# Conformer block on one core: GpSimd instead of VectorE computes the statistics of 15 LayerNorms

## The chip, the core and the metric

The kernel runs on one core of a Trainium2 chip. A core has TensorE (PE, matrix products into PSUM), VectorE (DVE), ScalarE (ACT), GpSimd (POOL) and SyncE (SP, which here only issues DMAs). The engines run side by side, each in the order of its own instruction list, and wait for each other on semaphores. The metric is the device time of one execution in microseconds; a change is told faster or slower here from 0.2% on.

## The reference

Input and output are 2 sequences of 4000 tokens with 144 channels, bf16. All weights are bf16; `_layernorm` takes mean and variance over the 144 channels and has no gain or bias.

```python
h = _layernorm(x);  x = x + 0.5 * (_silu(h @ w_ff1a) @ w_ff1b)      # 144 -> 576 -> 144
h = _layernorm(x);  q, k, v = split(h @ w_qkv)                     # 4 heads of 36
x = x + softmax(q k^T * 36**-0.5) v  @ w_o
h = _layernorm(x);  a, b = split(h @ w_pw1);  h = a * sigmoid(b)
x = x + _silu(depthwise_conv5(h)) @ w_pw2
h = _layernorm(x);  x = x + 0.5 * (_silu(h @ w_ff2a) @ w_ff2b)
return _layernorm(x)
```

So there are five LayerNorms for each token, and the attention over 4000 keys is most of the work.

## The kernel before

The 8000 tokens are 16 chunks of 500; a chunk is four blocks of 125 tokens, with tokens on the partitions. The running sum x stays in SBUF as `X`, bf16, [125 partitions, 64 blocks, 144].

**Attention.** For each chunk of queries the kernel walks over 63 tiles of 64 keys. PE makes the scores into two PSUM banks (`PS<-QT,KT`), then either ACT takes the exponential of both banks in one instruction (`ACT ... PT<-PS`), or DVE does it in five: two conversions from PSUM (`PT<-PS`, 128x500) and three steps within SBUF called y, m and w (`PT<-PT`: an and/or, a product of two tensors, an and/or). Then PE adds `PT` times the values to a sum in PSUM (`PS<-PT,VA`). 215 tiles are done by DVE, the others by ACT.

**Everything else** (feed-forward, projections, convolution, norms) is woven between these tiles. A norm is the function `ln(c, bs)`. For a whole chunk in the middle of the run it does the following: DVE issues two `bn_stats`, each over two blocks (125x288 bf16), which write count, mean and sum of squared deviations of each row into `ST`; GpSimd computes variance plus epsilon (`RS`), raises it to the power -0.5 (`NHALF`), negates the mean, and scales the four blocks of `X` into `XN` (125x144 each). After that SP issues a DMA transpose into `XTB`, from which PE multiplies, or, for the last norm of a chunk, the store to DRAM. `bn_stats` reads each pair of blocks interleaved, so that its two groups of three values are those of the two blocks.

**What sets the order.** The functions are coroutines that a planner runs with its own costs to make a first list of operations. Then `settle()` rewrites it by tables in the file: `UNITS` has one letter for each movable piece of work (`R.unit`), which says on which engine it runs (p for GpSimd, d for DVE, a for ACT), and `ORDER` gives for each engine the place of every step. `Rec.choose` applies the letters, `Rec.arrange` the order, `Rec.finish` finds the semaphore waits that are needed. The planner's costs so have no say in the final order. Instructions of one engine that depend on one another also wait on a semaphore. Since all are issued by one helper, every row of the profile carries the same line, L589.

Buffers that matter: `ST` and `RS` have five slots, as `XN`; `TH` holds the tanh tiles, six slots, of which two belong to `ff_wide` (two feed-forward tiles at once; the program as built has no such tile); `DWR` is a small buffer for the raw depthwise weights, used once near the start of the middle part (`setup_dw`).

Of the kernel before, what the change touches and what calls it, by code (L numbers as in the profile page):

```python
# [6 lines left out]
ALU = mybir.AluOpType  # L7
# [161 lines left out]
        '+8#v#y#z+9#{+5+:+;#|+<+=#}$!+>+?+@$#+A+B+C+D$&$$$%+E+F+G$(+H+J+I$)$*+K+O+L+P+M+N+Q$++T+R+U$,+S+V+Z+Y'
        '+W+X+[$-+]+^+_+`$.+a$/+e+b+d$0$3+f+c$4$1$2+g+j+i+k+h+l$6+m$7+n+o$5+p+s+q+t$8+u+x+v+r,!$9+w+}+y,,,#,&'  # L170
        ',-,$,%$:,.,($;,/,0+z,)$<+{+|$>$=,*,1$?,+,2,7,6,3,8,4,5$@$A,9,;,<,:,=,@,>,A$C,B,?,E,C,F,D,G,J$D$E,K$F'
        ',H,L,I$G,M,O,N,P$H,T$I,U,V$J,W$K,X,Q$L,R$M$N,S$O,Y$B,Z$P,[,_,],^$Q$R,`,a,d$S,e,b$T,c,f$U$V,i,g,j$W,k'
        ',n$X,h,l,o$Y,p,m,q$Z$[,s$],t,r,u,x$^,v,y$_,w,z,}$`,{-!$a-#-&$b-$-(,|-)-%-*-,$c---+-.$d-/-1-0$e-2-3$g'
        '-4$j$f-5$h-6$i-7-8-;$k-9-<$l-:-@-=$m$n-A->-B-E$o-?$p-C-F-D$q-G-J-H-K$r-O-I-L-P-M-Q$s-N-R-T$t-U-S-V-Y'
        '-W-X-Z$u-[-_-]-`-^$v-d-a-l-b-c-e$w-i-j-f-k-g-m-h$y-r-n-s-o-t-p-q$z${-u-v-w$|%)-x$}$x-y%!-z%,-{%#-|-}'
        '.!%$%%.%.&.(%&.).#.$%+%*.*%(.+%-%..,%/.-.0%0...1./%2%3%4%5.5.6.2.7.8.3.9.4.:%6.;%1.?.<%7.=.@%8.>.D.A'
        '%9.E.F%:.G.B.C%=%;%<.J.I.N%>.K.H.O%?%@.L.M%B.P%A.Q%C.T.S.R%D%F%E.U.X.V.Y.W.Z%G.[%H%I._.c.]%K.d.^%J.`'
        '.h.a%L.e%M.i.f.m%N.g%O.n.b.j.r.k.o.s.p%P.l%Q.w.q%R.x.}.y.|.z.t/%.u%S/&.{/+/!.v/,/#/(/$/)%T/0/5/*/-/.'
        '%U/1/6///2/7/3%V/4%W%X/8%Y/9%[%Z/?/:/@/;/<%^/A%`/B%_/=%a/>%b/C/D%c%]%e%d/E%f/F/I/G/J%g/H/O/N/K%h/S/L'
        '/P/Q/T%i/M/U/X/R/Y%j/V%k/W/Z/^/[%l/]%m/_/`/c/a/b%n/d/h/i/m/n/j/o/p/k/e%p/f%o/q/s/r/l/t/u/g/v%q%r/w/x'  # L180
        '0$0#%s0%/y/|%t/}0!0*0&/z%u0+/{0(0)0/%w040,%v050-%x060.00070801%y020:%z03%{090>0;%|0<0?0=0@%}0A0C0D0B'
        '&!0E&#0H0F&$0G&%0I0J&&0K0R0L0S&(0W0M0N0T0O0U0V0P&+&)&*0X0^0]0Q0_0Y0`0a&,0b0c0Z0d0[0e&-0g0f0h0m0l0q0i'
        '0r0n0j0o&.0v&/&00p0w0k0{0|0s0t0u&1&21$0}1!1#1%0x&30y&41&0z1(1/1)1+1*1,&61015111-1.&712&813&5141:1619'
        '171;181<1=&91?1>1C1D1@1E1A1B1I1H1F1G&;1J&:1K&<&>&=&?1R&@1L1M1N1O1S1P1T&A1Q1U1V1W1X&B1Y1]1^1Z1b1_1[1`'
        '1c&C1d1g1e1h1a1i1l1j1m&D1n1f1o&E1t1p&F1q1k1r1s&G&H&J&I&K1z1{1|&L&M1}1u1v2#2!1w2$1x1y2)&N&O2*2+2,2%2-'
# [8 lines left out]
        '5:(l5>55(k5A5?5F5@5B5E(p5G(o5C5P5D(q(i5H(m5O(n(t5U(r5Q5I(s(u5T5R5V5S5W5`5X5K5J5_5L5a5M5b(v(w5N5c5Y5Z'
        '5[5]5^(j(x)#(y(z)%({(})&(|)!)*))).)$)D)<)F)()=)>)+),)-)/)E)B)L)1)M)0);)?)I)@)2)N)C)4)5)3)G)7):)6)J)8'
        ')P)O)K)A)9)Q)H)U)V)R)S)T)Y)X)W)])Z)^)_)`)b)a)c)[)e)d)f)g)l)i)j)k)h)m'
# [124 lines left out]
class Rec:  # L321
# [441 lines left out]
def bass_standalone__conformer_family_zipformer__speech_kernel(  # L763
# [28 lines left out]
    def sb(name, shape, dt=BF16):  # L792
        return nc.alloc_sbuf_tensor(name, [128] + list(shape), dt)

    NXN, NXT, NTH, NHT, NSW = 5, 5, 6, 3, 3
# [27 lines left out]
        "FFW": (  # L823
# [4 lines left out]
        ),  # L828
# [140 lines left out]
    RS = sb("RS", [NXN, 3, NB], F32)  # L969
    NHALF = sb("NHALF", [NB], F32)  # L970
# [35 lines left out]
    DWR = sb("DWR", [D + 64])  # L1006
# [135 lines left out]
    def now(k):  # L1142
# [7 lines left out]
        Slots(R, range(n)) for n in (NXN, NXT, NTH - 2, NHT, NSW, NAN, NPT))  # L1150
    thw = Slots(R, [NTH - 2])
# [87 lines left out]
    def ln(c, bs, e=False, store=False):  # L1239
# [9 lines left out]
        calm = small(c)  # L1249
        if n == NB and not calm and not store and ("XN", u) not in clear:  # L1250
# [164 lines left out]
    def ff_wide(s, h, m, WA, nm):  # L1415
        bks, t = yield need("pe", (wide, thw), dur=0.84)
        for j in range(2):
            mm2(WA, s, (m + j) * 128, (m + j) * 128 + 128, bks[j], 128, [(nm, "a", 0)])
        yield need("act")
        rk = [("ps", bks[0]), ("ps", bks[1]), "TAB0"]  # L1420
        ps = PSV[:, bks[0]:bks[0] + 2, 0:CH]
        op("act", "activation", TH[:, t:t + 2, :], ps, ACT.Tanh, bias=0.0, scale=0.5, r=rk, w=[("TH", t)],
           cost=c_act(2 * CH))
        yield need("dve", hold=True)
        op("dve", "scalar_tensor_tensor", out=HT[:, h, m:m + 2, :], in0=TH[:, t:t + 2, :], scalar=1.0, in1=ps,
           op0=ALU.add, op1=ALU.mult, r=[("TH", t)] + rk, w=[("HT", h)], cost=c_dve(2 * CH))
        banks.give(bks[0])
# [1081 lines left out]
```

## Time and profile before

| what | value |
|---|---|
| median of 3 runs | 868.13 us (868.13 to 868.39) |
| profiled execution, time | 868.3 us |
| profiled execution, span from first to last instruction | 866.5 us |
| granted TensorE clock, mean | 0.998 |
| busy: PE, DVE, ACT, POOL | 849.1, 833.6, 835.0, 278.9 us |
| `bn_stats` on DVE | 160 instructions, 65.6 us |
| scaling into `XN` on POOL | 250 instructions, 141.6 us |

The profile's page gives busy times, the chain of work that ended last (followed back from the last instruction, at each step to what released it), and groups of equal instructions with their count, busy time, mean duration, and the engine's idle time just before them. Other views give the same for a window, or the instructions in order of time. An operand is written out<-in with the program's names.

### The profile page before, as it was taken

To read this page: it belongs to the slowest core of one execution; us is meant where nothing else is said; L and a number is where in the kernel's file an instruction comes from. 1 tells how busy PE (TensorE), PEld (TensorE's weight loads), DVE (VectorE), ACT (ScalarE), POOL (GpSimd) and SP (SyncE) were. 2 spreads that over 40 slices of the span, in tenths; PEclk is the share of its full clock that TensorE was granted. 3 is DMA by queue.
4 is the path that set the end of the run, shared out by engine and by line. 5 is a ranking of instruction groups with operands and counts; after the bars stand their busy time and mean duration, and the time that the engine had idled before them with its cause. 6 is when DMAs were issued, how large, how long until landed. Compare 5 with 4: busy or idle time off the path is not lost.

```text
span 866.5 us, 27023 instructions
## 1 busy us (share of the span) xinstructions
PE 849.1 (98%) x11585; PEld 411.2 (47%) x11585; DVE 833.6 (96%) x1819; ACT 835.0 (96%) x1096; POOL 278.9 (32%) x562
## 2 busy tenths in 40 slices
PE   9999999999999999999999999999999999999996
PEld 7644434444344444444444444444444544445485
DVE  7989999999999999999999999999999999999986
ACT  6999999999999999999999999999999999999975
POOL 7661331041334301432230060330550163300854
PEclk9999999999999999999999999999999999999999
DMA  3320211102113110212210020010130021100121
GB/s 103 87 56 14 33 21 38 21 14 45 34 26 51 14 26 2 40 31 45 34 39 2 2 44 3 17 29 14 27 47 6 5 54 37 29 2 14 36 51 51
DMA packets 86554, 26.95 MB, mean 31 GB/s; under 512 B 81607, under 2 KB 86433, under 8 KB 86433
## 3 DMA queue, kind: packets, MB, share of 16 engines
q1 hardware_dynamic: 84884, 24.38, 15.3%
q8 instruction: 91, 1.49, 0.7%
q10 hardware_dynamic: 1548, 0.84, 0.4%
q14 instruction: 31, 0.25, 0.1%
HBM read 3.34 MB, written 2.30 MB: 7 GB/s over the span
## 4 chain that ended last, share of the span: by engine, by line
ACT 40%; PE 40%; DVE 16%; DMA 1%; POOL 1%; issue 1%; DVEq 0%; POOLq 0%; ACTq 0%
PE PS L589 40%; ACT PT L589 37%; DVE PT L589 11%; ACT TH L589 3%; DVE ST L589 1%; DVE QT L589 1%; DVE X L589 1%; POOL XN L589 1%; DVE HT L589 1%; DVE U L589 1%; DMA XTB<-XN 0%; DMA X<-in_x_dram 0%; DMA out_dram<-XN 0%; DVE KT L589 0%; POOL RS L589 0%
## 5 line engine op out<-in xcount | busy, mean ns | idle before, releaser
L589 ACT ACTIVATE PT<-PS 128x1000 bf16<-128x1000 f32 (+1 forms) x793 | 730.2, 1070 | 5.3 <-PE PS L589 4.3
L589 PE MATMUL PS<-QT,KT 64*64 64x500 bf16 x3968 | 460.3, 383 | 4.3 <-ACT PT L589 1.2
L589 PE MATMUL PS<-PT,VA 64*37 64x500 bf16 x4828 | 449.5, 372 | 1.3 <-DVE QT L589 0.6
L589 DVE TENSOR_SCALAR PT<-PS 128x500 int16<-128x500 f32 x425 | 279.7, 678 | 4.4 <-PE PS L589 3.1
L589 PEld LDWEIGHTS PS<-QT,KT 64*64 64x64 bf16 x3968 | 139.7, 104 | 201.6 <-ACT PT L589 98.9
L589 PEld LDWEIGHTS PS<-PT,VA 64*37 64x37 bf16 x4828 | 163.1, 96 | 105.8 <-issue 16.4
L589 POOL TENSOR_SCALAR RS<-ST 125x4 f32<-125x4 f32 (+1 forms) x132 | 31.2, 238 | 482.2 <-DVE ST L589 478.5
L589 DVE TENSOR_SCALAR PT<-PT 128x1000 uint16<-128x1000 uint16 x430 | 172.3, 419 | 1.8 <-DVE PT L589 0.2
L589 DVE TENSOR_TENSOR PT<-PT 128x1000 bf16<-128x1000 bf16 x215 | 144.9, 678 | 0.8
L589 POOL TENSOR_SCALAR XN<-X,RS 125x144 bf16<-125x144 bf16 x250 | 141.6, 578 | 4.3 <-POOL RS L589 0.9
L589 POOL TENSOR_TENSOR RS<-RS,NHALF 125x4 f32<-125x4 f32 (+2 forms) x93 | 91.9, 993 | 53.5 <-DVE RS L589 51.4
L589 ACT ACTIVATE TH<-PS 128x500 bf16<-128x500 f32 (+3 forms) x175 | 92.8, 560 | 3.8 <-PE PS L589 3.4
L589 DVE SCALAR_TENSOR_TENSOR HT<-TH,PS 128x500 bf16<-128x500 bf16 (+1 forms) x120 | 71.7, 617 | 1.4 <-ACT TH L589 1.0
L589 PE MATMUL PS<-XTB,WA 72*128 72x500 bf16 (+2 forms) x280 | 71.1, 359 | 0.8 <-DMA XTB<-XN 0.2
L589 DVE BATCH_NORM_STATS2 ST<-X 125x6 f32<-125x288 bf16 (+1 forms) x160 | 65.6, 449 | 1.8 <-DMA X<-in_x_dram 1.1
L589 DVE SCALAR_TENSOR_TENSOR X<-PS,X 125x288 bf16<-125x288 f32 x114 | 50.9, 452 | 7.0 <-PE PS L589 5.9
L589 PE MATMUL PS<-WB,HT 128*125 128x144 bf16 (+1 forms) x640 | 52.2, 229 | 0.1
L589 PEld LDWEIGHTS PS<-WB,HT 128*125 128x125 bf16 (+1 forms) x640 | 45.0, 136 | 13.4 <-issue 3.9
L589 PEld LDWEIGHTS PS<-XTB,WA 72*128 72x128 bf16 x280 | 21.5, 97 | 29.0 <-issue 8.3
L589 PE MATMUL PS<-U,DG 128*128 128x375 bf16 (+7 forms) x204 | 28.0, 263 | 0.2 <-DVE RD L589 0.2
L589 POOL COPY U<-U 128x2 bf16<-128x2 bf16 (+1 forms) x54 | 10.8, 234 | 42.2 <-DVE U L589 32.1
L589 ACT ACTIVATE HT<-PS 128x500 bf16<-128x500 f32 (+3 forms) x43 | 20.6, 537 | 3.4 <-PE PS L589 2.9
(95 smaller groups left out, 513.9 us busy)
## 6 DMA issues: line engine op xcount, KB each, us to landing
X<-in_x_dram SPq DMA_DIRECT2D x16, 140.6 KB
XTQ<-XTB SPq DMA_DIRECT2D x24, 70.3 KB
out_dram<-XN SPq DMA_DIRECT2D x12, 140.6 KB
XTB<-XN SPq DMA_TRANSPOSE x53, 3.2
out_dram<-XN ACTq DMA_DIRECT2D x2, 140.6 KB
XTB<-AN SPq DMA_TRANSPOSE x15, 3.2
WA<-in_w_ff1a_dram ACTq DMA_DIRECT2D x1, 144.0 KB
WB<-in_w_ff1b_dram ACTq DMA_DIRECT2D x1, 144.0 KB, 2.6
```

What stands on the lines that cost most here:

```text
L589: ins = getattr(eng, o.name)(*o.a, **o.k)
```

## The change

In the LayerNorms of whole chunks in the middle part, a third letter, s, is now possible for the two `bn_stats`. With it DVE issues neither, and GpSimd makes the same two statistics (mean into `ST[..., 1]`, sum of squared deviations into `ST[..., 2]`) itself: it squares both halves of the 144 channels, adds the halves, adds the channels pairwise 72, 36, 18, 9 down to one, and corrects the sum of squares by the square of the sum over 144. Squares and plain sums go side by side as eight columns of 72 in `SQ`, fp32. 15 of the letters are s. The new list stands in GpSimd's order ahead of the `RS` instruction that reads `ST`.

The place for `SQ` and `SS` comes from `TH` (six slots to four; `ff_wide` is removed with its policy) and from `DWR`, which becomes a view of `SQ`; a norm can have the letter s only when `setup_dw` is done with that. The tables of PE, ACT and SP are untouched; those of DVE and POOL have new numbers, because the count of their steps changed, and name the remaining instructions in the order of before.

```diff
@@ Rec.choose
+                if code == "s":
+                    o.deps += [(x, True) for x in more]
                 more.append(o)
@@ buffers
-    NXN, NXT, NTH, NHT, NSW = 5, 5, 6, 3, 3
+    NXN, NXT, NTH, NHT, NSW = 5, 5, 4, 3, 3
+    SQ = sb("SQ", [2 * NB, HD], F32)
+    SS = sb("SS", [3, NB], F32)
-    DWR = sb("DWR", [D + 64])
+    DWR = SQ[:, :, :].rearrange("p i d -> p (i d)").bitcast(BF16)
@@ ln
+        seen = [(d, True) for j in range(n) for d in R.history(("X", c, b0 + j))[0]]
+        raws = []
         for j in range(0, n, 2):
-            op("dve", "bn_stats", ST[0:rows, u, j:j + 2, :].rearrange("p i k -> p (i k)"),
+            o = op("dve", "bn_stats", ST[0:rows, u, j:j + 2, :].rearrange("p i k -> p (i k)"),
...
+            raws.append(o)
         calm = small(c)
+        if n == NB and not calm and not e and R.history("DWR2")[1]:
+            seen += [(d, False) for q in ("DWR", "DWR2") for h in R.history(q) for d in h]
+            lo, hi = (X[0:TB, c * NB:c * NB + NB, q:q + HD] for q in (0, HD))
+            s1, s2, s3 = SS[0:TB, 1, :], SS[0:TB, 0, :], SS[0:TB, 2, :]
...
+            more = [(SQ[0:TB, NB:2 * NB, :], hi, hi, ALU.mult, 0.9), (SQ[0:TB, 0:NB, :], lo, lo, ALU.mult, 0.9),
+                    (SQ[0:TB, 0:NB, :], SQ[0:TB, 0:NB, :], SQ[0:TB, NB:2 * NB, :], ALU.add, 0.9),
+                    (SQ[0:TB, NB:2 * NB, :], lo, hi, ALU.add, 0.9), (z(0, 36), z(0, 36), z(36, 72), ALU.add, 0.9),
+                    (z(0, 18), z(0, 18), z(18, 36), ALU.add, 0.6), (z(0, 9), z(0, 9), z(9, 18), ALU.add, 0.42),
+                    (z(0, 3), z(0, 3), z(3, 6), ALU.add, 0.3), (z(0, 3), z(0, 3), z(6, 9), ALU.add, 0.3),
+                    (SS[0:TB, 0:2, :], col(0), col(1), ALU.add, 0.3),
+                    (SS[0:TB, 0:2, :], SS[0:TB, 0:2, :], col(2), ALU.add, 0.3), (s3, s1, s1, ALU.mult, 0.25)]
+            R.unit(raws, "d", {"s": [
+                ("pool", "tensor_scalar", (ST[0:TB, u, :, 1], s1, 1.0 / D, None), dict(op0=ALU.mult), 0.25, None),
+                ("pool", "tensor_tensor", (ST[0:TB, u, :, 2], s2, s3), dict(op=ALU.add), 0.25, None)]},
+                   {"s": [("pool", "tensor_tensor", (a, b, d), dict(op=f), t, None, None, seen) for a, b, d, f, t in more] + [
+                       ("pool", "tensor_scalar", (s3, s3, -1.0 / D, None), dict(op0=ALU.mult), 0.25, None, None, seen)]})
@@ ff: ff_wide removed
-        nw = 0 if silu or mode["front"] else now("FFW")
-        kids = S.spawn([ff_wide(s, h, 2 * j, WA, nm) for j in range(nw)] + [
-            ff_tile(s, h, m, WA, WE, nm, silu) for m in range(2 * nw, 5)])
+        kids = S.spawn([ff_tile(s, h, m, WA, WE, nm, silu) for m in range(5)])
```

(The last numbers in the rows of `more` are the planner's costs.)

More of the change, by code (lines that the diff above doesn't have):

```diff
@@ L169 @@
[L169 to L173, printed above, removed]
@@ L194 @@
[L194 to L196 removed]
+        '#,#-#.#V)_)`#/)a)b#0#1)d)e#2)f)i)g#4)c#3#5)h)j)k)l#7#6#W)t)n)m)o)s)p#8)q#9)u#:)v)w)r#<)x)y)})z#;#=*!'
+        '){*#)|*(*$#>*&*%#?*)#@***+*,*-*1*.#A*/*0#B*2*3#C#D#F*6#E*4*7*5#G#H*;#I*8*9*<*=*:*>*?#J*A*@*E*F*B#K#L'
@@ new lines @@
+        '#M*C*D#N#Y*J*G#O#P#R*K#Q#S*H#^*L#T#X*I*M#Z*N*P#[#_*O*Q#]*R*S#a*U#`*T#b#c*V*Y*W*Z*X*[#e*_*]#f#g*^*`#h'
+        '*a#i*b*d#j*c*e#d#k*f*j*g*i*h*k#m*l#l*m#n#p*n*o*s#o*p*x#q*q*y*t*}*u*r#r*v#s*z#t+!#u*w+&*{*|+#+$#v#w+('
+        '+)#x#y+*#z+%+++,#{+-+.#|#}+/+0+1$!+2+3+4+5$%$#$$+6+7+8$&+9+;+:$($)+<+@+=+A+>+?+B$*+E+C+F$++D+G+K+J+H'
+        '+I+L$,+M+N+O+P$-+Q$.+U+R+T$/$2+V+S$3$0$1+W+Z+Y+[+X+]$4+^$5+_+`+a+d+b+e$6+f+i+g+c+o$7+h+n+j+x+p+s+y+q'
+        '+r$8+z+t$9+{+|+k+u$:+l+m$<$;+v+}$=+w,!,(,&,#,),$,%$>$?,*,,,-,+,.,1,/,2$@,3,0,6,4,7,5,8,;$A,<$B,9,=,:'
@@ L197 @@
+        '4D4E(G4F(I4G4:4H(J4J4K4L4I(K4O4M4N4P4T4Q(L4R4U4S4V4Y4W(M4_4`4X4a4Z4b4c4[4e(N4]4d4^4f4g(O4j4h4i(Q4k4l'
+        '(P4m(R(S4o4n4p(T4q(U(V4s4t4u4r4v4w(W(X4y4x5(4z4}4{4|5-5&5,5!5)5#5*5.5$5+(]5/5%([525057515356(a58(`54'
+        '5A55(b(Y59(^5@(_(e5F(c5B5:(d(f5E5C5G5D5H5P5I5<5;5O5=5Q5>5R(g(h5?5S5J5K5L5M5N(Z(i(p(j(k(r(l(n(s(m(o(v'
+        '(u(z(q)5)-)7(t).)/(w(x(y({)6)3)=(})>(|),)0):)1)!)?)4)$)%)#)8)()+)&);)))A)@)<)2)*)B)9)F)G)C)D)E)J)I)H'
+        ')M)K)N)O)P)R)Q)S)L)U)T)V)W)])Y)Z)[)X)^'
     ),
@@ L206 @@
+        '#Y#[#a#b#f#c#`#k#d#g#e#m#i#l#n#o#p#r#q#s#x#y#}#z#t#{$+#|$$$&$!#w$)#u$#$%#v$($*$,$-$.$:$4$2$3$/$0$5$8'
+        '$6$7$1$9$;$<$=$A$>$B$C$?$D$E$G$F$@$I$H$J$K$L$Q$S$U$O$T$P$V$W$X$Y$M$_$]$N$Z$[$^$a$e$c$R$b$d$f$`$g$h$j'
+        '$i$n$r$p$q$s$t$u$v$k$x$y$w$l$z${$m$|$o%!%#%$%%%&%(%*%)%+$}%,%-%.%/%1%0%2%3%4%5%6%<%=%>%7%?%8%@%D%E%A'
+        '%:%G%F%9%H%;%B%I%C%K%L%J%O%U%R%V%M%W%X%S%N%P%Q%T%Y%Z%]%^%[%_%`%a%b%c%d%f%e%g'
     ),
@@ L1149, in bass_standalone__conformer_family_zipformer__speech_kernel @@
     xnp, xtp, thp, htp, swp, anp, ptp = (
-        Slots(R, range(n)) for n in (NXN, NXT, NTH - 2, NHT, NSW, NAN, NPT))
-    thw = Slots(R, [NTH - 2])
+        Slots(R, range(n)) for n in (NXN, NXT, NTH, NHT, NSW, NAN, NPT))
     wide = Wide(banks)
@@ L1413, in ff_tile @@
         thp.give(t)
[L1415 to L1427, printed above, removed]
-        banks.give(bks[1])
-        thw.give(t)
     def ff(c, s, WA, WE, WB, nm, silu, then):
         h = yield need("pe", htp)
-        nw = 0 if silu or mode["front"] else now("FFW")
-        kids = S.spawn([ff_wide(s, h, 2 * j, WA, nm) for j in range(nw)] + [
-            ff_tile(s, h, m, WA, WE, nm, silu) for m in range(2 * nw, 5)])
+        kids = S.spawn([ff_tile(s, h, m, WA, WE, nm, silu) for m in range(5)])
         yield need("pe", kids=kids)
```

69 lines of the change are left out of this document (32 added, 37 removed), and 4 rows, old and new, of the table POLICY.

## The prediction

> **What bounds the kernel now.** I read the page first (busy shares, the chain that ended last, the costliest groups), then busy time by stretch, then the chain in the stretches where the change acts, then single tiles and timelines.
>
> ```profile
> span 866.5 us, 27023 instructions
> PE 849.1 (98%) x11585; PEld 411.2 (47%) x11585; DVE 833.6 (96%) x1819; ACT 835.0 (96%) x1096; POOL 278.9 (32%) x562
> ACT 40%; PE 40%; DVE 16%; DMA 1%; POOL 1%; issue 1%; DVEq 0%; POOLq 0%; ACTq 0%
> L589 DVE TENSOR_SCALAR PT<-PT 128x1000 uint16<-128x1000 uint16 x430 | 172.3, 419 | 1.8 <-DVE PT L589 0.2
> L589 DVE TENSOR_TENSOR PT<-PT 128x1000 bf16<-128x1000 bf16 x215 | 144.9, 678 | 0.8
> L589 DVE BATCH_NORM_STATS2 ST<-X 125x6 f32<-125x288 bf16 (+1 forms) x160 | 65.6, 449 | 1.8 <-DMA X<-in_x_dram 1.1
> XTB<-XN SPq DMA_TRANSPOSE x53, 3.2
> ```
>
> Three engines are full at once, and the chain changes between them: 40% of it is ScalarE's (ACT), 40% TensorE's (PE), 16% VectorE's (DVE). GpSimd (POOL) has two thirds of the span free. In the body, by stretch:
>
> ```profile
> 40.00:820.00 780.00, 772.04 (x10720) 351.37 (x10718) 763.73 (x1599) 771.51 (x963) 228.29 (x453) 1.00 0.15 27
> ```
>
> The columns are PE, its weight loads, DVE, ACT, POOL. ACT is idle for 8.5 of 780 us, DVE for 16.3. ACT's share cannot shrink, since the change takes nothing from it; so no relief of DVE can give more than ACT's idle time there.
>
> **What the change removes.** 15 norms lose their two bn_stats on DVE: 30 x 449 ns = 13.5 us of DVE's 833.6. The orders of PE, ACT and SP stay as they are, and so does DVE's but for the missing 30; the wide feed-forward tile that goes is issued nowhere, and the smaller TH and the move of DWR into SQ add no instruction: nothing for them, by that order.
>
> **What it adds.** 15 GpSimd instructions a norm, 225 in all: five of 288 elements, one of 144, one of 72, two of 24, two of 8, four of 4. The trace has no addition of two tensors on GpSimd, so I bound it.
>
> ```profile
> L589 POOL TENSOR_SCALAR XN<-X,RS x250: 452/460/1740, 16.1 to 857.2; 125x144 bf16<-125x144 bf16 x125
> L589 POOL MEMSET XN<- x5: 465/471/472, 17.7 to 71.1; 128x448 bf16 x5
> L589 POOL TENSOR_SCALAR RS<-ST x132: 187/221/699, 5.5 to 855.6; 125x4 f32<-125x4 f32 x113, 125x2 f32<-125x2 f32 x18, 126x2 f32<-126x2 f32 x1
> 145.25 0.20 POOL L589 TENSOR_SCALAR RS<-ST 125x4 f32<-125x4 f32 x1 [22.76 <-DVE ST L589]
> 145.53 1.01 POOL L589 TENSOR_TENSOR RS<-RS,NHALF 125x4 f32<-125x4 f32 x1
> ```
>
> The first three rows give min/median/max in ns. From below, an instruction that only writes: 471/448 = 1.05 ns an element, 0.30 us for 288. From XN, which reads one tensor: (460-187)/140 = 1.95 ns an element over a fixed 187 ns, 0.74 us for 288. From above, that slope twice, for two tensors read in full: 1.29 us. I take 0.80 us, close to XN, the nearest row (same engine, same rows of X, two arithmetic steps), a little over it for the second operand. [...]
>
> At 2.16 ns an element over 187 ns (0.80 us for 288), a norm costs 5 x 0.80 + 0.49 + 0.33 + 2 x 0.23 + 2 x 0.20 + 4 x 0.19 = 6.4 us; each instruction waits for the one before it, and such a wait costs 0.08 us (145.25 + 0.20 to 145.53), 14 times: 7.6 us (about 4.6 to 10.4 between the ends). GpSimd goes from 279 to about 393 us busy, 45%.
>
> **Does anyone wait for the later statistics?** Today GpSimd waits for them:
>
> ```profile
> POOL RS L589 <- DVE ST L589: 478.5, 58, 35.9
> ```
>
> That is 478.5 us in 58 waits, 8.2 us each, and the new work starts in that idle time, as soon as the chunk is written and GpSimd is free. For the 15 places that is at 155.7, 197.2, 222.1, 241.0, 273.4, 298.9, 323.3, 360.0, 401.5, 429.3, 473.8, 530.3, 592.7, 667.0 and 785.3 us. In about half of them the statistics are then ready before bn_stats ended, in the others up to 7 us later. The tightest place is the eighth:
>
> ```profile
> 360.94 0.81 DVE L589 BATCH_NORM_STATS2 ST<-X 125x6 f32<-125x288 bf16 x2
> 363.15 2.54 POOL L589 TENSOR_SCALAR XN<-X,RS 125x144 bf16<-125x144 bf16 x4
> 369.00 1.27 SPq L589 DMA_TRANSPOSE XTB<-XN  x1
> 380.08 0.58 PE L589 MATMUL PS<-XTB,WA 72*128 72x500 bf16 x2
> ```
>
> The block ends at 360.0 + 7.6 = 367.6 instead of 361.75, 5.9 us late. The XN behind it in GpSimd's queue (of another chunk) ends at 371.6, SP's transpose goes out at 371.6 instead of 369.0, lands 3.2 us later (page row above) at 374.8, and PE uses it at 380.08: 5.3 us to spare. SP has nothing else to issue until this has landed. So the added latency is put at nothing; it is hidden by GpSimd's idle time and this slack.
>
> **The cost on VectorE.** GpSimd and VectorE get in each other's way:
>
> ```profile
> 441.45 0.90 POOL L589 TENSOR_SCALAR XN<-X,RS 125x144 bf16<-125x144 bf16 x2
> 442.05 0.83 DVE L589 TENSOR_TENSOR PT<-PT 128x1000 bf16<-128x1000 bf16 x1
> L589 DVE TENSOR_SCALAR PT<-PT x430: 365/414/690, 56.6 to 820.1; 128x1000 uint16<-128x1000 uint16 x144
> L589 DVE TENSOR_TENSOR PT<-PT x215: 627/672/859, 57.2 to 819.4; 128x1000 bf16<-128x1000 bf16 x108
> ```
>
> The product at 442.05 began with 0.30 us of a GpSimd instruction to go (441.45 + 0.90 = 442.35) and took 0.83 us instead of the median 0.672: it lost what was left of that instruction less 0.15 us. What this costs now: mean less median, (419-414) x 430 + (678-672) x 215 = 3.4 us, against 250 x 0.460 = 115 us of undisturbed XN, so 3.0%. An instruction of length T makes a VectorE one that starts at random lose (T-0.15)^2/2T: 0.104 us for XN, 0.264 for 0.80 us, 2.5 times. So 7.6% of 15 x (4.0 + 0.49 + 0.33) = 72 us: **5.5 us of lock losses** on VectorE. (At 0.30 us an instruction: 0.3 us; at 1.29: 16.7.) The short instructions, about 0.2 us, cost next to nothing.
>
> [...]
>
> **What reaches the end.** Two of the 15 pairs lie on the chain, 0.73 us each:
>
> ```profile
> 289.52 1.46 DVE ST L589 x4
> 432.55 0.73 DVE ST L589 x2
> by line: DVE PT L589 74.2%; PE PS L589 17.4%; DVE HT L589 6.5%; DVE X L589 4.1%; issue 0.5%
> by line: ACT PT L589 41.0%; DVE PT L589 25.7%; PE PS L589 21.1%; ACT TH L589 5.3%; DVE AN L589 5.1%; issue 3.4%; DVE RD L589 2.7%
> by line: DVE PT L589 80.4%; PE PS L589 13.2%; DVE U L589 10.0%; issue 1.0%
> by line: DVE PT L589 52.6%; DVE ST L589 16.2%; DVE QT L589 11.2%; DVE VA L589 6.6%; DVE KT L589 6.5%; DVE HT L589 6.5%; DVE X L589 4.3%; issue 1.0%
> 155.70:164.70 9.00, 9.00 (x146) 3.93 (x140) 8.90 (x20) 9.00 (x11) 1.45 (x3) 1.00 0.16 31
> ...
> 785.30:794.30 9.00, 9.00 (x144) 4.89 (x138) 9.00 (x19) 9.00 (x12) 0.20 (x1) 1.00 0.16 32
> sum 135.00, PE 133.54 PEld 58.09 DVE 133.15 ACT 134.97 POOL 18.29; mean PE 8.90 PEld 3.87 DVE 8.88 ACT 9.00 POOL 1.22
> ```
>
> Two of the four instructions at 289.52 are of a norm that moves. The four "by line" rows are the chain in 222.1:231.1, 298.9:307.9, 401.5:410.5 and 429.3:438.3, the only ones of the 15 stretches (9 us each) in which it runs over DVE: 85%, 34%, 90% and all, 28 of 135 us. The last rows are busy times over the 15 stretches (first, last and sum): DVE is idle for 1.85 us of 135, ACT for 0.03.
> - Gain: 2 x 0.73 = -1.46 us. The other 13 pairs are off the chain; taking them out frees DVE, and nobody was waiting there.
> - Loss on the chain: 5.5 x 28/135 = +1.1 us.
> - Loss elsewhere: 4.4 us in stretches where ACT has no idle time. DVE's own idle time there, 1.85 x 107/135 = 1.5 us, takes its part; the rest delays what PE gets from DVE, and ACT through PE, and an engine without idle time does not make that up: +2.9 us.
>
> Sum: +2.5 us on the profiled execution's 868.3 us, which lies 0.2 us over the median of 868.13: **870.6 us**, slower by 0.3%. Between the ends of the lock losses it would be -1.4 us (0.3 us lost, all of it hidden) to +13.8.
>
> **The rivals.** *The relief reaches the end (faster).* DVE is freed of 13.5 - 5.5 = 8.0 us. TensorE waits for it, and ACT for TensorE:
>
> ```profile
> PEld PS L589 <- DVE PT L589: 72.7, 239, 0.6
> ACT PT L589 <- PE PS L589: 4.3, 13, 0.6
> ACT TH L589 <- PE PS L589: 3.4, 10, 1.4
> ```
>
> If a third of the 8.0 us comes out of ACT's 8.5 us of idle time in the body, that is -2.7 us, 865.4. It decides from 1.7 us on (0.2% of 868, about what a measurement can tell from no change). For it: 239 waits of weight loads on DVE's exponentials. Against: near the removed pairs ACT is not idle at all.
> *Hidden (no change).* The losses off the chain fall into DVE's waits: -1.46 + 1.1 = -0.4 us, 867.7. For it: at most 0.4 us per block. Against: DVE's 0.12 us of idle time a stretch.
> *GpSimd comes too late (slower).* It decides when a block takes 7.6 + 5.3 = 12.9 us, beyond the upper end; each us more is then a us of PE's wait at 380. At 15 us: +2 on top, 872.7.
> That the change does nothing is excluded: in the built program bn_stats go from 160 to 130, and GpSimd gains 225 instructions.
>
> **How the numbers follow.** Forecast (losses pass): 0.50, of which 0.06 at small losses stay within 0.2%; relief reaches the end: 0.25; hidden: 0.21; too late: 0.04. So faster 0.25, same 0.27, slower 0.48. The range reaches down past a third of the relief, 865.0, and up to twice the losses (11 us: -1.46 + 2.3 + 7.2 = +8.0), 876.3. The forecast's own range is 868.5 to 876.3.
>
> **What would show it.** DVE busy falls by 8 us (13.5 less 5.5), PT<-PT means rise from 419 and 678 ns to about 426 and 690 (430 x 7 + 215 x 12 = 5.6 us), medians stay; the 288-element rows take 0.80 us; GpSimd's waits for DVE ST shrink; ACT's idle time in the body grows by 2 to 3 us. Wrong: if those means stay, if ACT's idle time falls under 8, or if PE waits for XTB at 380.

## The result, and the profile after

The changed kernel takes 879.33 us (median of 4 runs, 879.28 to 879.52) against 868.26 us for the kernel before in the same session: a ratio of 1.0127 (95% interval 1.0109 to 1.0144), slower by 1.3%. The prediction said slower, but by 0.3%, and 879.3 lies outside its range. The profiled execution's span is 877.5 us, at the same granted clock as before (0.998).

The page of the changed kernel: busy times, the chain that ended last by engine, and the costliest groups that matter here (group rows: out<-in, shapes, count | busy us, mean ns | idle before them).

```profile
span 877.5 us, 27220 instructions
PE 852.3 (97%) x11585; PEld 411.0 (47%) x11585; DVE 840.5 (96%) x1789; ACT 837.8 (95%) x1096; POOL 392.4 (45%) x787
...
PE 42%; ACT 30%; DVE 27%; issue 1%; DMA 0%; POOL 0%; DVEq 0%; ACTq 0%
...
L592 DVE TENSOR_SCALAR PT<-PT 128x1000 uint16<-128x1000 uint16 x430 | 183.3, 444 | 2.1 <-PE PS L592 0.6
L592 DVE TENSOR_TENSOR PT<-PT 128x1000 bf16<-128x1000 bf16 x215 | 150.7, 705 | 0.8
L592 DVE BATCH_NORM_STATS2 ST<-X 125x6 f32<-125x288 bf16 (+1 forms) x130 | 53.5, 448 | 1.6 <-DMA X<-in_x_dram 0.9
```

GpSimd went from 279 to 392 us (forecast: 393). VectorE should have come down by 8 us; it went up by 7, from 833.6 to 840.5, although 30 `bn_stats` are gone. The two `PT<-PT` groups took that back and more: their means rose from 419 to 444 ns and from 678 to 705 ns (forecast: 426 and 690). VectorE's share of the chain went from 16% to 27%.

One tile's rows (min/median/max in ns) show that the instructions as such are what they were; it is the longest that grew, from 690 and 859 ns:

```profile
L592 DVE TENSOR_SCALAR PT<-PT x430: 368/414/1050, 56.5 to 832.0; 128x1000 uint16<-128x1000 uint16 x144
L592 DVE TENSOR_TENSOR PT<-PT x215: 626/672/1549, 57.1 to 831.2; 128x1000 bf16<-128x1000 bf16 x108
```

Mean less median, (444-414) x 430 + (705-672) x 215, is 20.0 us. It was 3.4 us before, so 16.6 us are new. The work that GpSimd gained, shapes kept apart:

```profile
L592 POOL TENSOR_TENSOR SQ<-X 125x288 f32<-125x288 bf16 x45 | 34.5, 767 | 136.7 <-DVE X L592 113.2 <-ACT X L592 21.2
L592 POOL TENSOR_TENSOR SQ<-SQ 125x288 f32<-125x288 f32 x30 | 27.6, 919 | 2.4
L592 POOL TENSOR_TENSOR SQ<-SQ 125x144 f32<-125x144 f32 x15 | 8.2, 546 | 1.2
L592 POOL TENSOR_TENSOR SQ<-SQ 125x72 f32<-125x72 f32 x15 | 5.7, 383 | 1.2
```

The five 288-element instructions take 0.77 and 0.92 us, 0.83 on the mean (the shortest 0.66 and 0.79): the forecast's 0.80 was near. Who waits (waiting engine and tile <- what it waited for: us, times, longest):

```profile
POOL RS L592 <- DVE ST L592: 226.9, 42, 22.8
PEld PS L592 <- DVE PT L592: 86.1, 253, 1.8
ACT PT L592 <- PE PS L592: 12.7, 26, 1.5
```

GpSimd's wait for `bn_stats` halves, from 478.5 us. What grows is what stands behind VectorE: weight loads waiting for its exponentials (72.7 to 86.1 us), and ScalarE's exponentials waiting for TensorE (4.3 to 12.7 us). In the body ScalarE is now idle for 791.0 - 773.5 = 17.5 us, where it was 8.5:

```profile
40.00:831.00 791.00, 774.13 (x10711) 350.31 (x10713) 769.66 (x1568) 773.45 (x961) 340.70 (x676) 1.00 0.14 26
```

(Columns: PE, weight loads, DVE, ACT, POOL.) A single loss looks like this, in order of time:

```profile
227.35 0.85 POOL L592 TENSOR_TENSOR SQ<-SQ 125x288 f32<-125x288 f32 x1
...
227.47 1.27 DVE L592 TENSOR_TENSOR PT<-PT 128x1000 bf16<-128x1000 bf16 x1
```

The GpSimd addition ends at 227.35 + 0.85 = 228.20. VectorE's product, begun at 227.47, takes 1.27 us instead of 0.67: it lost 0.60 of the 0.73 us that were left. The trace has 35 `PT<-PT` instructions that ran beside a wide sum and took over 25 ns more than their median; 34 of them lost what was left of the sum less 0.13 to 0.14 us.

Since ScalarE's order is untouched, the start of its n-th exponential can be set against the same one before, which shows where the time went. The table is worked out from the traces (start after, less start before, us; relief, powers and few are experiments below):

```
start before   changed   relief   powers    few
156.4           -0.2       0.3      0.8     0.0
176.0            0.9       0.3      0.8     0.0
216.4            1.9       0.3      0.8    -0.1
236.2            4.0       0.4      0.8    -0.1
276.7            5.2       0.4      0.8     0.0
336.8            8.0      -0.1      0.0    -0.5
395.0            7.8      -0.1      0.2    -0.5
434.6            9.1       0.5      0.4     0.8
532.6           10.9       0.5      0.4     0.9
608.7           11.5       0.7      0.6     0.9
808.7           11.9       0.5      0.3     1.3
```

The delay climbs where the norms with GpSimd's sums lie (eight of the fifteen between 155 and 361 us), stands still between them, and is never made up.

### The profile page after: what moved, and what is told of

Read it like the earlier page. It is cut to its first block, busy times and chain, and to the rows that moved or that the text cites. A ratio compares the mean times of both kernels' runs of the same rounds, so it can differ in the third digit from the quotient of the medians.

```text
span 877.5 us, 27220 instructions
## 1 busy us (share of the span) xinstructions
PE 852.3 (97%) x11585; PEld 411.0 (47%) x11585; DVE 840.5 (96%) x1789; ACT 837.8 (95%) x1096; POOL 392.4 (45%) x787
## 4 chain that ended last, share of the span: by engine, by line
PE 42%; ACT 30%; DVE 27%; issue 1%; DMA 0%; POOL 0%; DVEq 0%; ACTq 0%
PE PS L592 42%; ACT PT L592 27%; DVE PT L592 20%; ACT TH L592 2%; DVE HT L592 1%; DVE ST L592 1%; DVE QT L592 1%; DVE X L592 1%; DVE U L592 1%; DMA X<-in_x_dram 0%; DVE KT L592 0%; DVE AN L592 0%; DVE XN L592 0%; POOL RS L592 0%; DVE VA L592 0%
## 5 line engine op out<-in xcount | busy, mean ns | idle before, releaser
L592 ACT ACTIVATE PT<-PS 128x1000 bf16<-128x1000 f32 (+1 forms) x793 | 730.4, 1054 | 13.8 <-PE PS L592 12.7
L592 DVE TENSOR_SCALAR PT<-PT 128x1000 uint16<-128x1000 uint16 x430 | 183.3, 444 | 2.1 <-PE PS L592 0.6
L592 DVE TENSOR_TENSOR PT<-PT 128x1000 bf16<-128x1000 bf16 x215 | 150.7, 705 | 0.8
L592 POOL TENSOR_SCALAR RS<-ST 125x4 f32<-125x4 f32 (+1 forms) x132 | 33.1, 253 | 231.7 <-DVE ST L592 226.9
L592 POOL TENSOR_TENSOR SQ<-X 125x288 f32<-125x288 bf16 x45 | 34.5, 767 | 136.7 <-DVE X L592 113.2
L592 ACT ACTIVATE TH<-PS 128x500 bf16<-128x500 f32 (+3 forms) x175 | 90.9, 548 | 4.5 <-PE PS L592 4.1
L592 DVE BATCH_NORM_STATS2 ST<-X 125x6 f32<-125x288 bf16 (+1 forms) x130 | 53.5, 448 | 1.6 <-DMA X<-in_x_dram 0.9
L592 POOL TENSOR_TENSOR SQ<-SQ 125x288 f32<-125x288 f32 (+2 forms) x90 | 50.0, 556 | 7.1
L592 PEld LDWEIGHTS PS<-WB,HT 128*125 128x125 bf16 (+1 forms) x640 | 45.0, 136 | 13.5 <-issue 4.3
```

The source lines that it names most:

```text
L592: ins = getattr(eng, o.name)(*o.a, **o.k)
```

## The experiments

Three theories for the 11 us stood at first. Theory 1: GpSimd's wide instructions hold up VectorE's `PT<-PT` (what the prediction calls lock losses, at three times the forecast 5.5 us; the traces show who is held up and for how long, not by what). Theory 2: GpSimd is late with the norms, and somebody waits. Theory 3: taking `bn_stats` out, or the smaller `TH` and the shared `SQ`, does harm by itself. All runs were timed beside the kernel before on the same chip; ratios are to it.

**Relief alone** (`relief`). `bn_stats` are gone, and GpSimd writes constants instead of the sums. Theories 1 and 2 had 864 to 868 us here, theory 1 with the `PT<-PT` means back at 418 to 421 and 677 to 682 ns.

```diff
-            more = [(SQ[0:TB, NB:2 * NB, :], hi, hi, ALU.mult, 0.9), ...]
-                   {"s": [("pool", "tensor_tensor", (a, b, d), dict(op=f), t, None, None, seen) for a, b, d, f, t in more] + [...]})
+                   {"s": [("pool", "memset", (SS[0:TB, 0:1, :], 1.0 * D), {}, 0.1, None, None, seen),
+                          ("pool", "memset", (SS[0:TB, 1:3, :], 0.0), {}, 0.1, None, None, seen)]})
```

> The changed kernel without the sums: VectorE's 30 bn_stats are gone as in the change, and GpSimd writes constants in place of the sums (two memsets, then the change's own last two instructions on 4 elements, which write mean 0 and variance 1 times 144 into ST). The 15 norms thus leave x unscaled; all else, order and buffers, is the changed kernel's. [...] Theory 3 (the removal itself, a late arrival of work that bn_stats held back, or the smaller TH and the shared SQ buffer make the loss): 876 to 880 us.

868.04 us, ratio 0.9994 (0.9985 to 1.0004). The removal does no harm, and it brings nothing that can be measured. VectorE's loss is back near that of before (the first mean 2 ns under what theory 1 had):

```profile
L592 DVE TENSOR_SCALAR PT<-PT 128x1000 uint16<-128x1000 uint16 x430 | 171.4, 416 | 2.1 <-PE PS L592 0.6
L592 DVE TENSOR_TENSOR PT<-PT 128x1000 bf16<-128x1000 bf16 x215 | 145.3, 680 | 0.8
```

**Work alone** (`work`). VectorE keeps its `bn_stats`; GpSimd makes the sums too, and nobody reads them. Theory 1 had 880 to 885 us here, theory 2 877 to 881.

```diff
-            R.unit(raws, "d", {"s": [
+            R.unit(raws, "d", {"b": [(o.eng, o.name, o.a, o.k, 0.365, None) for o in raws], "s": [
-                   {"s": [("pool", "tensor_tensor", (a, b, d), ...) for a, b, d, f, t in more] + [...]})
+                   {"b": [("pool", "tensor_tensor", (a, b, d), ...) for a, b, d, f, t in more] + [...] + last})
-                o.deps = o.deps + [(x, True) for x in more]
+                o.deps = o.deps + [(x, True) for x in more] * (code != "b")
```

(`last` is the change's last two instructions, writing to a spare place.)

> The other half alone: VectorE keeps its 30 bn_stats where they were, and GpSimd makes all 15 norms' sums with the change's own instructions, at the change's places in its order, into a place that nobody reads; TH and SQ as changed. [...] Theory 3: 868 to 869 us if the removal is what hurts, 876 to 880 if the buffers do.

880.78 us, ratio 1.0147 (1.0128 to 1.0165). The whole loss of time is there without any removal. VectorE's two groups (theory 1 had a mean of 440 to 446 ns for the first):

```profile
L592 DVE TENSOR_SCALAR PT<-PT 128x1000 uint16<-128x1000 uint16 x430 | 181.1, 438 | 1.8 <-DVE PT L592 0.2
L592 DVE TENSOR_TENSOR PT<-PT 128x1000 bf16<-128x1000 bf16 x215 | 148.8, 696 | 0.8
```

Together with `relief` this rules out theory 3's removal. Mean less median is 17.6 us here, 13.6 over the 4.0 of `buffers` (below), which also keeps its `bn_stats`; the time is up by 12.8 us (11.1 to 14.3). So with `bn_stats` in place little of the loss, if any, is hidden.

**The same lateness without wide instructions** (`powers`).

```diff
-            more = [(SQ[0:TB, NB:2 * NB, :], hi, hi, ALU.mult, 0.9), ...]
+            extra = [("pool", "memset", (SP4[0:TB, 0:1, :], 1.0), {}, 0.1, None, None, seen)] + [
+                ("pool", "tensor_tensor", (p1[:, 0:w], p0[:, 0:w], nh[:, 0:w]), dict(op=ALU.pow), 1.0, None, None, seen) for w in (4, 4, 4, 4, 4, 2, 1)] + [
+                ("pool", "tensor_tensor", (s3, p1, p1), dict(op=ALU.mult), 0.25, None, None, seen)] * 6
```

> The changed kernel with the same lateness but without wide instructions on GpSimd: each norm's sums are replaced by seven pow instructions on 1 to 4 elements (about 1 us each by their time in the kernel before), six multiplications of 4 elements and memsets, some 9 us in a chain, and constants as in the run with memsets; the 15 norms leave x unscaled. Theory 1: within 1.5 us of the run with memsets, 864 to 869 us, PT<-PT means at 418 to 422 and 677 to 683 ns. Theory 2: as the changed kernel, 876 to 880 us. Theory 3: 876 to 880 us.

867.70 us, ratio 0.9991 (0.9982 to 1.0001). GpSimd is busier here than in the changed kernel (425 against 392 us), its blocks are longer, and VectorE loses nothing:

```profile
PE 849.7 (98%) x11585; PEld 411.4 (48%) x11585; DVE 824.9 (95%) x1789; ACT 834.6 (96%) x1096; POOL 425.0 (49%) x832
L592 POOL TENSOR_TENSOR SP<-SP,NHALF 125x4 f32<-125x4 f32 x75 | 82.7, 1102 | 6.0
L592 DVE TENSOR_SCALAR PT<-PT 128x1000 uint16<-128x1000 uint16 x430 | 171.6, 416 | 2.1 <-PE PS L592 0.7
L592 DVE TENSOR_TENSOR PT<-PT 128x1000 bf16<-128x1000 bf16 x215 | 144.9, 678 | 0.8
```

Theory 2 falls. So does any theory by which a busy GpSimd as such slows VectorE: 75 two-tensor `pow` on 4 elements, 1.1 us each, cost nothing that can be measured.

**Buffers alone** (`buffers`). All letters back to d, so that only the smaller `TH` and the shared `SQ` are left.

```diff
(the tables, in words)
-UNITS with 15 letters s, ORDER of the changed kernel
+UNITS with d in their place, ORDER of the kernel before
```

> The changed kernel with bn_stats back on VectorE for all 15 norms and nothing added on GpSimd: only TH with 4 buffers in place of 6 and SQ in DWR's place are left of the change. Theories 1 and 2: 868.0 to 868.6 us, as before. Theory 3: 870 us or more if the buffers are the cause.

868.90 us, ratio 0.9999 (0.9990 to 1.0009), as before (868.70 beside it). Theory 3 is out, and theory 1 is left. But why do the sums cost so much more than the scaling into `XN`, from which the prediction took its price? I counted VectorE's `PT<-PT` instructions that took over 25 ns more than the median, by the GpSimd instruction that ran then. In the changed kernel: 35 beside `XN` (of its 250), 139 ns each; 35 beside the 75 wide sums, 420 ns each. The two differ in number for two reasons in about equal part: 142 of the 250 `XN` run beside no `PT<-PT` at all, against 14 of the 75 sums, and of those that do meet one, 35 of 108 hold it up, against 35 of 61. The next runs ask what makes a sum so dear.

**One tensor instead of two** (`one_input`). The nine widest instructions of a norm become `tensor_scalar` of the same shape and chain; constants as in `relief`. Theory 1a, that two tensors are what makes a sum dear, while an instruction with one mostly waits for VectorE, had 867 to 870 us, with means up to 424 and 686 ns.

```diff
-            more = [(SQ[0:TB, NB:2 * NB, :], hi, hi, ALU.mult, 0.9), ...]
+            extra = [("pool", "tensor_scalar", (o, i, 0.5, None), dict(op0=ALU.mult), 0.9, None, None, seen) for o, i in (
+                (SQ[0:TB, NB:2 * NB, :], hi), (SQ[0:TB, 0:NB, :], lo), (SQ[0:TB, 0:NB, :], SQ[0:TB, 0:NB, :]),
+                (SQ[0:TB, NB:2 * NB, :], lo), (z(0, 36), z(0, 36)), (z(0, 18), z(0, 18)), ...)]
```

> The changed kernel with each of a norm's nine widest GpSimd instructions (five of 288, then 144, 72 and two of 24 elements) made a one-input tensor_scalar of the same shape, chained by the same waits; constants stand in for the statistics, so the 15 norms leave x unscaled. [...] Theory 1b (the length of the instruction or the wait that each carries sets the loss): 875 to 880 us, means 435 to 446 and 695 to 706 ns.

869.75 us, ratio 1.0013 (1.0004 to 1.0023). The loss is a third of the changed kernel's (4.9 against 15.0 us, both over `relief`), though these instructions are longer, 0.93 us at the least against 0.66 with two tensors:

```profile
L592 POOL TENSOR_SCALAR SQ<-X x45: 927/985/1350, 156.1 to 790.5; 125x288 f32<-125x288 bf16 x45
L592 DVE TENSOR_SCALAR PT<-PT 128x1000 uint16<-128x1000 uint16 x430 | 175.5, 426 | 2.0 <-PE PS L592 0.6
L592 DVE TENSOR_TENSOR PT<-PT 128x1000 bf16<-128x1000 bf16 x215 | 146.6, 686 | 0.8
```

So the length that the profile gives a GpSimd instruction is not what VectorE pays for: 1b falls (it had 875 us or more; the first mean is 2 ns over what 1a had). Three rows in order of time, from two windows of this trace (the first `PT<-PT` alone, then both together): the second of the two ends at 238.90 + 0.97 = 239.87, while the GpSimd instruction runs until 238.97 + 1.18 = 240.15. VectorE finished inside it:

```profile
238.90 0.41 DVE L592 TENSOR_SCALAR PT<-PT 128x1000 uint16<-128x1000 uint16 x1
...
238.90 0.97 DVE L592 TENSOR_SCALAR PT<-PT 128x1000 uint16<-128x1000 uint16 x2
238.97 1.18 POOL L592 TENSOR_SCALAR SQ<-X 125x288 f32<-125x288 bf16 x1
```

**Wide instructions apart** (`apart`). A narrow `pow` behind each wide one, so that they no longer stand back to back; the narrow steps are left out, and constants stand in for the statistics.

```diff
+                extra += [... 
+                    ("pool", "tensor_tensor", (o, a, b), dict(op=f), 0.9, None, None, seen),
+                    ("pool", "tensor_tensor", (SP4[0:TB, 1, :], SP4[0:TB, 0, :], NHALF[0:TB, 0:NB]), dict(op=ALU.pow), 1.0, None, None, seen)]
```

> [...] Theory 1c (back to back, a wide instruction that VectorE has held up slips in as VectorE's instruction ends, delays the next, and so they alternate: the loss comes from standing back to back): VectorE loses under 8 us, 867 to 873 us. Theory 1d (each wide instruction costs its own share wherever it starts): 16 us lost as in the change, 876 to 880 us.

877.32 us, ratio 1.0099 (1.0084 to 1.0114), means of 439 and 693 ns: mean less median 17.5 us. Theory 1c falls: a wide instruction cost nearly its share without another right behind it (35 hold-ups of 373 ns on the mean, against 35 of 420 beside the changed kernel's wide sums).

**A chain of waits, and none** (`bf_chain`, `bf_free`). Five two-tensor instructions that read X and write bf16: chained, and with the first four free of each other. Theory 1e, that the wait of each on the one before is what makes the sums dear, had 867 to 872 us for the free ones, with under half of their partner's loss.

```diff
+            extra = [("pool", "tensor_tensor", (o, a, b), dict(op=f), 0.9, None, None, seen) for o, a, b, f in (
+                (q(0), hi, hi, ALU.mult), (q(1), lo, lo, ALU.mult), (q(2), lo, hi, ALU.mult), (q(3), lo, hi, ALU.add), (q(0), lo, hi, ALU.add), ...)]
@@ bf_free only
-                    o.deps += [(x, True) for x in more]
+                    o.deps += [(x, len(more) >= 4) for x in more]
```

> Each norm has five 288-element tensor_tensor instructions that read only X and write bf16, each waiting for the one before as in the change, then 72, 36 and 12 elements; constants stand in for the statistics, so the 15 norms leave x unscaled. It is the partner of the next run. Theory 1a (two tensors) and 1e (the wait of each on the one before): 875 to 880 us, PT<-PT means 435 to 446 and 695 to 706 ns. If fp32 output or fp32 input is what costs: 867 to 870 us.

> As the run with bf16 sums, but the first four of the five 288-element instructions write four places and wait for nothing of each other. [...] Theory 1a (two tensors, wait or no wait): within 1.5 us of its partner, 875 to 880 us.

Chained 878.14 us, ratio 1.0112 (1.0095 to 1.0129); free 884.98 us, ratio 1.0184 (1.0166 to 1.0203). Theory 1e is refuted: without the waits VectorE loses more, not less (19.0 against 13.8 us over `relief`). In the run without them, the groups and one place in order of time:

```profile
L592 DVE TENSOR_SCALAR PT<-PT 128x1000 uint16<-128x1000 uint16 x430 | 183.0, 443 | 2.1 <-PE PS L592 0.6
L592 DVE TENSOR_TENSOR PT<-PT 128x1000 bf16<-128x1000 bf16 x215 | 153.3, 717 | 0.8
```

```profile
440.09 1.97 POOL L592 TENSOR_TENSOR SQ<-X 125x288 bf16<-125x288 bf16 x3
440.06 3.23 DVE L592 TENSOR_TENSOR PT<-PT 128x1000 bf16<-128x1000 bf16 x1
```

Three GpSimd instructions from 440.09 to 442.06, a fourth behind them, and VectorE's product of 0.67 us takes 3.23: it got its turn after all four. So back to back without a wait they can hold VectorE off from the first to the last. They do not always: in this trace it happened twice (2.56 and 2.39 us lost), and none of the other hold-ups beside wide instructions cost more than 0.55 us, about as in `bf_chain`, where the longest cost 0.67. Those two make up most of the 5.2 us by which VectorE lost more here than in `bf_chain`. What decides whether VectorE gets in between is open. fp32 output or input is not what costs either, since `bf_chain` loses nearly as much as the changed kernel (13.8 against 15.0 us).

**The partner with one tensor** (`bf_one`): as `bf_chain`, with `tensor_scalar`.

```diff
-            extra = [("pool", "tensor_tensor", (o, a, b), dict(op=f), 0.9, None, None, seen) for o, a, b, f in (
+            extra = [("pool", "tensor_scalar", (o, a, 0.5, 0.25), dict(op0=ALU.add, op1=ALU.mult), 0.9, None, None, seen) for o, a in (
```

> The partner of the run with bf16 sums in a chain: the same five 288-element instructions, chained, reading X and writing bf16, but each a tensor_scalar that reads one tensor (x plus a constant, times a constant, the form of the x normalization), the three narrow ones as there; constants stand in for the statistics, so the 15 norms leave x unscaled. It parts the number of tensors from the pace: in the earlier run the one-tensor instructions also wrote fp32 and took 0.93 us at the least, against 0.66 with two tensors. Theory 1a (one tensor gives way to VectorE): VectorE loses at most 6 us more than without sums, single losses of at most about 0.3 us beside those of x normalization, 868.5 to 871 us. If a slow pace or the fp32 output is what gave way: 875 to 879 us, single losses of 0.4 us and more.

871.80 us, ratio 1.0034 (1.0021 to 1.0046), a little over the range of 1a. The wide instructions lose VectorE 4.7 us where the two-tensor partner lost about 13, by the count above. But the rows correct the reading that one tensor "gives way":

```profile
L592 POOL TENSOR_SCALAR SQ<-X x75: 425/431/1512, 155.9 to 791.2; 125x288 bf16<-125x288 bf16 x75
L592 DVE TENSOR_SCALAR PT<-PT 128x1000 uint16<-128x1000 uint16 x430 | 176.4, 428 | 2.0 <-PE PS L592 0.6
L592 DVE TENSOR_TENSOR PT<-PT 128x1000 bf16<-128x1000 bf16 x215 | 147.1, 689 | 0.8
```

An undisturbed one takes 0.43 us, against 0.66 with two tensors. Where it held VectorE up longest, VectorE was 0.32 us late, which is again what was left of it less 0.15 us: it did not give way, it was shorter. The 0.93 us in `one_input`, with the same 0.32 us as the longest loss, are in two parts by its trace. VectorE's instructions that began early in one had their turn 0.50 to 0.55 us before its end, which leaves some 0.43 us of hold. In the last 0.36 us the two forms of `PT<-PT` part:

```profile
598.25 0.93 POOL L592 TENSOR_SCALAR SQ<-X 125x288 f32<-125x288 bf16 x1
598.83 0.62 DVE L592 TENSOR_SCALAR PT<-PT 128x1000 uint16<-128x1000 uint16 x1
...
532.54 1.07 POOL L592 TENSOR_SCALAR SQ<-X 125x288 f32<-125x288 bf16 x1 [11.01 <-DVE X L592]
533.26 0.67 DVE L592 TENSOR_TENSOR PT<-PT 128x1000 bf16<-128x1000 bf16 x1
```

Both began with 0.35 us to go (598.25 + 0.93 less 598.83; 532.54 + 1.07 less 533.26). The and/or step took 0.62 us instead of 0.41, so it lost what was left less 0.14; the product took its 0.67 and lost nothing. All 10 and/or steps that began with 0.16 to 0.36 us to go behave like the first, all 8 products like the second. So the end of such an instruction holds VectorE's and/or steps and not its products; why, the runs do not show.

**In pieces** (`pieces`, `pieces_chain`). The change's own sums with each 288-element instruction cut into four of 72; free of each other within a step, and chained. Theory 1f, that two-tensor instructions without a wait between them hold VectorE off from the first to the last (it had lost 2.56 us at one place in `bf_free`), had 877 to 884 us for the free pieces, with single losses of 0.5 us and more; theory 1g, that VectorE gets in at the end of each, 869 to 873 us and at most 0.25 us each.

```diff
+            def cut(o, a, b, f):
+                return [(o[:, j:j + 1, :], a[:, j:j + 1, :], b[:, j:j + 1, :], f, 0.3) for j in range(NB)]
+            more = cut(SQ[0:TB, NB:2 * NB, :], hi, hi, ALU.mult) + cut(SQ[0:TB, 0:NB, :], lo, lo, ALU.mult) + ...
@@ pieces only
-                    o.deps += [(x, True) for x in more]
+                    o.deps += [(x, k < len(more) // 4 * 4 or len(more) >= 20) for k, x in enumerate(more)]
```

> The change with each 288-element instruction of a norm cut into four of 72 elements (20 in place of 5), the four of one step without waits between them, the steps chained; the same statistics. [...]

> [...] Theory 1f and 1g both: single losses of at most about 0.25 us (72 elements took 0.38 us in the change, less the 0.15), twice as many of them at most, 4 to 8 us lost on VectorE's PT<-PT beyond the 4.3 us of before, 870 to 873 us, provided that the longer block, about 11 us, is hidden as the 13 us block of the run with pow between was. If the loss goes by the GpSimd time spent on two tensors and not by the length of one instruction: 877 us or more.

Free pieces 873.63 us, ratio 1.0065 (1.0050 to 1.0080); chained 871.76 us, ratio 1.0043 (1.0028 to 1.0057). The chained ones came out as expected. The free ones lie between 1f and 1g: two losses of about 0.8 us, each over four pieces in a row, but the others stay under 0.26 us. Chained, with GpSimd busiest of all (448 us):

```profile
L592 POOL TENSOR_TENSOR SQ<-X x180: 298/319/1523, 155.7 to 794.8; 125x72 f32<-125x72 bf16 x180
L592 DVE TENSOR_SCALAR PT<-PT 128x1000 uint16<-128x1000 uint16 x430 | 178.1, 432 | 2.1 <-PE PS L592 0.6
L592 DVE TENSOR_TENSOR PT<-PT 128x1000 bf16<-128x1000 bf16 x215 | 146.9, 687 | 0.8
```

**Five norms of fifteen** (`few`). VectorE lost 2.2 us to these five in the changed kernel. At its ratio of time to loss (11.6 us for 16.6, 0.70), less a third of the 0.7 us that `relief` gained, that made 869 to 870.5 us.

```diff
(the tables, in words)
-15 letters s
+5 letters s (the norms at 368, 409, 438, 678 and 797 us), d for the other ten
```

> The change for 5 of the 15 norms alone (the 8th, 9th, 10th, 14th and 15th in time, at 368, 409, 438, 678 and 797 us), which lost VectorE 2.2 of the 14.7 us of the wide instructions; the other ten as before. [...] If the place of the norm doesn't matter, a third of the whole: 871.5 to 873 us.

869.14 us, ratio 1.0014 (1.0004 to 1.0024). The place of a norm decides: these are a third of the norms, and VectorE's loss is an eighth (1.8 of 15.0 us over `relief`). They were picked as the cheap ones from the changed kernel's trace.

The runs side by side, cheapest first; loss is mean less median over the two `PT<-PT` groups of each profile, hold-ups are the counted losses to the sums' instructions, time is the ratio less that of `relief`, on 868.7 us (a profile is one execution, and the kernels with no sums at all range from 3.4 to 5.0 us of loss, so a difference of a microsecond says little):

```
kernel         shortest wide   hold-ups, mean ns     loss   over relief   time over relief
relief              -               -                 5.0       -              -
few              0.66 us          10, 247             6.8      1.8            1.7
one_input        0.93             37, 144             9.9      4.9            1.7
bf_one           0.43             40, 164            11.4      6.4            3.5
pieces_chain     0.30             70, 114            12.2      7.2            4.3
pieces           0.30             80, 120            14.1      9.1            6.2
apart            0.66             35, 373            17.5     12.5            9.1
bf_chain         0.66             36, 385            18.8     13.8           10.3
changed kernel   0.66             45, 352            20.0     15.0           11.6
bf_free          0.66             40, 485            24.0     19.0           16.5
```

With all 15 norms the time is the loss less about 3 us (2.5 to 3.5), over a range of 5 to 19 us: so much is hidden, and the rest comes through whole. VectorE's idle time is where most of it would go: span less busy time is 40.6 us in `relief` and 37.0 in the changed kernel. But `bf_free`, with 2.5 us hidden, has 40.5, so this is a reading and not shown. With these orders no cheaper way of making the sums can beat the kernel before by a measurable amount: `relief`, which makes none at all, is at 0.9994.

## Why the prediction was wrong

**What failed: the price of the lock losses.** The term "7.6% of 72 us: 5.5 us" measured 16.6 us, 14.7 of them counted beside the wide sums. That the sums hold VectorE up was right, the size was not. The term was built as `XN`'s rate, 3.0%, times 2.5 for the length, with VectorE's instruction one that "starts at random". Per wide sum that comes to 0.061 us, or 0.23 hold-ups of 0.264 us; measured were 0.47 hold-ups of 0.42 us. So both factors were too small. How often: `XN` holds VectorE up in 35 of 250 instructions, 14%; the wide sums in 35 of 75, 47%. How long: VectorE's instructions do not start at random. 23 of the 35 hold-ups come from sums that began while an earlier `PT<-PT` still ran, so that VectorE's next one came while most of the sum was still to go; these lost 0.47 us on the mean, the other 12 lost 0.32. The price of the length was unsound too, though it did no harm: a one-tensor instruction of 288 elements needs 0.43 us when it writes bf16 (`bf_one`), no more than `XN` with 144 (0.45), so the slope of 1.95 ns an element, drawn through `XN` and a 4-element row, is no price for another shape. For two tensors the 0.80 us was near all the same, by luck. (It is 2.13 ns an element over 187 ns, not 2.16; nothing hangs on it.) Why `XN` holds VectorE up so seldom, with instructions as long as `bf_one`'s, is only in part answered by its meeting fewer `PT<-PT`; the rest is open, since the runs did not vary `XN`. The range had the same fault. It stretched the instruction's length (0.30 to 1.29 us) and kept the rate, so that the true loss met only the extreme end, "At 1.29: 16.7", which the final range cut off at 11 us.

**What held.** That VectorE "lost what was left of that instruction less 0.15 us" is seen again (0.60 of 0.73 us, and 34 of 35 hold-ups beside wide sums at 0.13 to 0.14). So it is for the instructions of 0.43 and 0.66 us, less 0.13 to 0.15 us; not for the 0.93 us ones of `one_input`, inside which VectorE could finish (at 239.87, with 0.28 us to go).

**The added latency "at nothing"** was right: `powers`, with longer blocks, is at 0.9991, and in the changed kernel TensorE's weight loads wait 0.9 us for `XTB` in the whole span, as before, and not at the tight place. TensorE did wait for GpSimd behind a sum once, 1.4 us at 308 us; the chain runs over VectorE there.

**What reaches the end** was nearly right. Its steps with 16.6 us in place of 5.5 give 16.6 x 28/135 = 3.4 on the chain, 13.2 - 1.5 = 11.7 elsewhere, less 1.46: +13.6 us, against +11.0 measured. The 1.5 us that VectorE's idle time would hide are about 3 in the runs, by whatever way.

**The gain of 1.46 us** does not show: `relief` is at -0.5 us (-1.3 to +0.3), within what can be told from no change. VectorE's busy time did fall there, from 833.6 (`buffers`, same chip) to 825.5 us, and nobody was waiting for it, as the prediction said of 13 of the 15 pairs. That is 8.1 us with hardly any loss to set against it, not 13.5. Part of the difference is that neighbours on VectorE overlap in the trace, which 30 x 449 ns counts as relief (at the 0.73 us of a pair on the chain it is 11.0 us for 15); the rest is open.

**The rivals.** The relief that "reaches the end" is refuted by `relief` itself: even with no loss at all, VectorE's freed time brings nothing. "Too late" is refuted by `powers`. "Hidden" holds for some 3 us of loss, not for 16.6. Of the marks, the means rose as said but two to four times as far (25 and 27 ns instead of 7 and 12), GpSimd's waits shrank as said, ScalarE's idle time grew by 9 us and not by 2 to 3, and VectorE's busy time rose where a fall was forecast. GpSimd's busy time came out (392 for 393 us) by luck: the forecast counted 14 waits of 0.08 us a norm as busy time, and the new instructions took 7.5 us a norm where it had 6.4.

## What to carry to other kernels

Work moved to an idle engine was not free here, where the engine that it was taken from runs 645 short `PT<-PT` instructions (0.41 and 0.67 us) within SBUF: a hold-up cost what was left of GpSimd's instruction less 0.13 us, 47% of the wide ones caused one, and only about 3 us of all the losses were hidden. Price such a collision from instructions of the same shape and number of tensors, count how often they collide as well as for how long, and let the range vary the rate, not only the length. If GpSimd must share the time, short instructions with a wait between them cost a third of wide ones here (+3.7 us against +11.0 for the same sums), and instructions of 4 elements cost nothing that could be measured (`powers`, ratio 0.9991).

## What the runs showed of the hardware beyond the forecast

- Two-tensor GpSimd instructions without a wait between them can hold VectorE off from the first to the last: 3.23 us for a product of 0.67 us, 2.81 us for an and/or step of 0.41 (`bf_free`).
- 75 `pow` of 4 elements, 1.1 us each, cost VectorE nothing (`powers`, means of 416 and 678 ns, as in `relief` within 2 ns): the time of an instruction alone did not tell what it cost VectorE.
- A `tensor_scalar` over 288 elements takes 0.43 us from bf16 to bf16 (an addition and a product) and 0.93 us from bf16 to fp32 (a product), and the second holds VectorE up no longer than the first (longest loss 0.32 us in both). The second holds twice, though: VectorE's and/or steps that began in its last 0.36 us waited for its end (all 10), its products did not (all 8).
